# One reciprocal square root on ScalarE for a logarithm and an exponential, in an attention and MLP kernel under a planned order

## The chip, the cores and the metric

The kernel runs on one core of a Trainium2 chip. The metric is the device time of one execution in microseconds (us). Before the change the median of three runs is 662.1 us (660.76 to 663.17).

## The reference

A complex linear attention is followed by an MLP. There are 4 batches of 8 heads, 768 steps and a head width of 48. The transition of each step is a complex number per element, scaled so that its magnitude is at most 0.999:

```python
mag = np.sqrt(a_re * a_re + a_im * a_im)
scale = np.minimum(mag, 0.999) / (mag + 1e-06)
a_re_n, a_im_n = (a_re * scale, a_im * scale)
for t in range(S):
    new_re = ar * S_re - ai * S_im          # S_re, S_im: 48 x 48 per head
    new_im = ar * S_im + ai * S_re
    S_re, S_im = (new_re + k[t] v[t]^T, new_im)
    y[t] = q[t] @ S_re
x = y as 3072 tokens x 384
out = gelu(x @ w_in) @ w_out                # w_in 384 x 2048, w_out 2048 x 384
```

## The kernel before

The recurrence is worked out in chunks. The running products of the transitions are needed for every step. They are computed on 128 lanes, in 24 slices of 8 rows (9 rows in the last slice of a group). The slices form four groups, `lanes0` to `lanes3`, of 4, 4, 8 and 8 slices. A row is 48 numbers, so a slice's tile is 128x384, or 128x432 with 9 rows.

A slice has two phases. In phase a, `squares_a` squares both parts into `tab` (a ring of one buffer), their sum is made in `sum_of` (by TensorE for slices 1 to 5, otherwise by VectorE), `logs` makes the reciprocal magnitude r from the sum and the square of r, and `normalise` improves r by one Newton step and scales the transitions. Then `scan` multiplies the rows one after the other: two VectorE instructions per row, `tt` and `bt`. In phase b, one slice later, `squares_b`, `sum_of` and `logs` make the reciprocal squared magnitude of the products, and `towards` and `against` multiply keys and queries by the products into `xt`. `xt` goes to DRAM (`kq`) and comes back in another layout (`kqn`) for `unit`, which does the attention of 128 steps of a batch on TensorE (`att`) and makes a 128-token piece of the MLP's input `xT`. There are 24 units.

Both MLP weights come as 64-bit floats. Each is cut into 16 pieces of 128x384, and `weights` turns a piece into two 32-bit halves (`wi_hi`, `wi_lo`, `wo_hi`, `wo_lo`): on VectorE six instructions or so through `wh` and `raw`, on ScalarE a square and a sign with sums (checks of the range) and two copies, on TensorE three matmuls. `block` is the MLP on 2 or 3 units at a time, nine of them; it walks over 16 pieces f of the hidden layer: nine matmuls into `ph`, two Gelus on ScalarE (`gh`, `gf`), a subtraction on VectorE (`gl`), and matmuls into `po`.

No engine's order is written out by hand. All steps go into a `Plan`. `natural` ranks each step by the work that still hangs on it, plus a constant of its kind (`MORE`), where each VectorE step of a slice's scan counts `WL`-fold along the chain of scans. `forward` simulates the engines with fixed costs and takes the step of the highest rank that is ready; `BIAS` leans the choice where a step may run on one of two engines (`both`, `either`). `order` repeats this up to four times with ranks taken from a backward pass and keeps the shortest plan. `issue` then writes every engine's instructions in that order, and each engine works through its own list strictly in it. The lines of the profile are therefore nearly all L429, the line that records a step, and groups are told apart by tile names.

ScalarE needs the table set of a function loaded. `TABLES` names the set of each function for the plan; `issue` loads the set at L427 where it changes, L422 loads the first one, and the loads before Gelu have L429.

The change touches `TABLES`, `FIRST_TABLE`, `WL`, `MORE`, `BIAS` and `logs`.

Of the kernel before, what the change touches and what calls it, by code (L numbers as in the profile page):

```python
# [15 lines left out]
AF = mybir.ActivationFunctionType  # L16
# [66 lines left out]
ENTER, LEAVE = dict(narrow=0.09), dict(narrow=0.2, turn=0.075)  # L83
STAY = 1.0
COLD, WARM = 3.0, 4.0
TABLES = {AF.Ln: "natural_log_exp_and_others", AF.Exp: "natural_log_exp_and_others", AF.Gelu: "gelu"}
FIRST_TABLE = TABLES[AF.Ln]
NEAR = 0.076
LOCK = True
NGA, NGB = 6, 5  # L90
# [4 lines left out]
EARLIER, N_RAW, N_KP = 1, 4, 2  # L95
PASSES = 4
N_A = 4
WL = 4.532

MORE = dict(lanes0=483.83, lanes1=-1595.06, lanes2=-3639.85, lanes3=-3453.18, weights=-1624.01, units=-66.21, blocks=-85.66)  # L100
BIAS = dict(vector=-0.82, scalar=-1.94, gpsimd=0.93, sync=-6.23)


class Step:
# [8 lines left out]
class Plan:  # L113
# [57 lines left out]
    def add(self, calls):  # L171
# [4 lines left out]
        for call in calls:  # L176
# [9 lines left out]
            for x in tuple(call[2]) + tuple(call[3].values()):  # L186
                step.table = TABLES.get(x, step.table) if isinstance(x, AF) else step.table
            for x, writes in [(x, False) for x in ins] + [(x, True) for x in outs]:
# [85 lines left out]
    def natural(self):  # L274
# [4 lines left out]
        for i in range(len(steps) - 1, -1, -1):  # L279
# [9 lines left out]
            rest[i] = t  # L289
        return [t + MORE[s.kind] for t, s in zip(rest, steps)]  # L290

    def forward(self, rank):
# [6 lines left out]
        free = dict.fromkeys(FIXED, 0.0)  # L299
        table = FIRST_TABLE  # L300
        channel, flight = dict.fromkeys(FIXED, 0.0), []
# [5 lines left out]
        while len(order) < len(steps):  # L307
            best = None
            for e, waiting in pool.items():
# [8 lines left out]
                if len(steps[i].options) > 1:  # L318
                    ends = {o: max(free[o], ready[i], port[other[o]] if o in steps[i].port else 0.0) + c + BIAS[o] for o, (_, c) in steps[i].options.items()}
                    if ends[e] > min(ends.values()) + 1e-9:  # L320
# [99 lines left out]
    def issue(self):  # L420
        table = FIRST_TABLE
        self.nc.scalar.preload_act_table_set(table)  # L422
        for s in self.order():
            if s.table and s.table != table:
                table = s.table
                if table != "gelu":
                    self.nc.scalar.preload_act_table_set(table)  # L427
            for engine, name, args, kw in s.calls:
                getattr(getattr(self.nc, engine), name)(*args, **kw)  # L429
# [10 lines left out]
def lanes_and_chunks(ctx, tc, flags, a_lanes, x_lanes, v_units, w_in, w_out, out):  # L440
# [5 lines left out]
    P = Plan(nc, loose=[flags])  # L446
# [12 lines left out]
    sgn, tiny, low_w, sj = (by_partition[:, i:i + 1] for i in range(4))  # L459
# [82 lines left out]
    tiles, xs = {}, {}  # L542
# [59 lines left out]
    def logs(sb, sa):  # L602

        with P.together():
            if sb is not None:
                P.scalar.activation(tiles[sb]["te"], tiles[sb]["b2"], AF.Ln, bias=tiny)
            if sa is not None:
                P.scalar.activation(tiles[sa]["tb"], tiles[sa]["a2"], AF.Ln, bias=tiny)
            if sb is not None:
                P.scalar.activation(tiles[sb]["te"], tiles[sb]["te"], AF.Exp, scale=-1.0)  # L610
            if sa is not None:
                P.scalar.activation(tiles[sa]["tb"], tiles[sa]["tb"], AF.Exp, scale=-0.5)
        if sa is not None:
            P.scalar.activation(tiles[sa]["tc"], tiles[sa]["tb"], AF.Square, accum_out=flags[:, sa:sa + 1])

# [76 lines left out]
    def lanes_begin():  # L692
        for s in range(N_A):
            load_a(s)
        load_x(0)
        load_x(1)
        squares_a(0)
        logs(None, 0)
        normalise(0)
        squares_a(1)  # L700
        logs(None, 1)

    def tick(s):
# [10 lines left out]
        with P.work(part=f"a{s}"):  # L714
            if ahead is not None:
                squares_a(ahead)
            if g == 0:
                if back is not None:
                    logs(back, None)
                if ahead is not None:  # L720
                    logs(None, ahead)
            elif back is not None or ahead is not None:
                logs(back, ahead)
# [367 lines left out]
    def ticks(g):  # L1091
        P.chain["vector"] = "lanes", WL
        with P.work(f"lanes{g}"):
            for s in range(end):
                if slices[s][0] == g:
                    tick(s)
        P.chain.pop("vector")
# [255 lines left out]
```

## Time and profile before

| | us |
|---|---|
| median of three runs (lowest, highest) | 662.1 (660.76, 663.17) |
| span of the profiled execution | 659.6 |
| TensorE matmul busy | 614.1 (93%) |
| TensorE weight load busy | 563.8 (85%) |
| VectorE busy | 484.1 (73%) |
| ScalarE busy | 434.1 (66%) |
| GpSimd busy | 26.1 (4%) |

The span runs from the first instruction to the last; what lies around it is in the runs and not in the span, 2.5 us against the median. Busy TensorE time is that of pipelined matmuls whose ends are modelled. All times in the trace are from the start of the span. PE is TensorE, PEld its weight loads, DVE VectorE, ACT ScalarE, POOL GpSimd, SP SyncE.

### The profile page before, as it was taken

The page shows a single profiled execution, that of the slowest core. Times are in us where ns is not written, and L with a number is a line of the kernel's source. Part 1 is how long each engine was busy: PE and PEld are TensorE (multiplying, and loading weights), DVE is VectorE, ACT ScalarE, POOL GpSimd, SP SyncE. Part 2 cuts the span into 40 slices and gives each one's busy share as a digit, 9 for nine tenths or more (in the row PEclk, how much of TensorE's full clock was granted, in tenths as well). Part 3 has the DMA queues.
Part 4 walks back from the last instruction along what each step waited for, and adds up shares of the span by engine and source line. Part 5 has one row for each costly group of instructions (what it writes and reads, how often), then busy time and mean ns, then how long its engine had stood idle before and what let it go on. Part 6 is the DMA issues. An engine that isn't in the chain of part 4 may idle for free.

```text
span 659.6 us, 13997 instructions
## 1 busy us (share of the span) xinstructions
PE 614.1 (93%) x5154; PEld 563.8 (85%) x5154; DVE 484.1 (73%) x1204; ACT 434.1 (66%) x1107; POOL 26.1 (4%) x74
## 2 busy tenths in 40 slices
PE   4655499999999999999999999999999999999995
PEld 2322277988789999999999999999999999999995
DVE  6999999999999999999989999656334424232211
ACT  8976699999998979787476997535442422232332
POOL 1000100002000000120000000020000000000000
PEclk9787699999999999999999999999999999999999
DMA  9366876668266456687889966487444132110000
GB/s 322 119 158 161 256 225 212 185 196 258 71 197 173 116 135 177 163 173 158 198 198 219 230 157 166 116 167 169 104 88 88 50 64 46 34 51 15 25 1 27
DMA packets 210442, 93.51 MB, mean 142 GB/s; under 512 B 167744, under 2 KB 202688, under 8 KB 210368
## 3 DMA queue, kind: packets, MB, share of 16 engines
q1 hardware_dynamic: 210368, 92.57, 54.6%
q8 instruction: 41, 0.67, 0.4%
q14 instruction: 33, 0.27, 0.1%
HBM read 63.11 MB, written 25.69 MB: 135 GB/s over the span
## 4 chain that ended last, share of the span: by engine, by line
PE 70%; ACT 9%; DVE 9%; issue 2%; DMA 1%; SPq 0%; DVEq 0%; ACTq 0%
PE po L429 27%; PE ph L429 26%; PE att L429 17%; DVE a L429 2%; ACT a L429 1%; DVE tt L429 1%; ACT tab L429 1%; ACT L429 1%; ACT L427 1%; DVE xt L429 1%; ACT gh L429 1%; DVE bt L429 1%; ACT gf L429 1%; DMA raw<-in_w_pieces_dram 1%; ACT square L429 1%
## 5 line engine op out<-in xcount | busy, mean ns | idle before, releaser
L429 PE MATMUL ph<-xT,wi_hi 128*128 128x384 f32 (+1 forms) x864 | 209.2, 324 | 0.0
L429 DVE TENSOR_TENSOR gl<-gf,gh 128x384 fp32r<-128x384 f32 (+1 forms) x144 | 73.7, 512 | 126.4 <-ACT gf L429 126.0
L429 ACT ACTIVATE gh<-ph 128x384 fp32r<-128x384 f32 (+1 forms) x144 | 65.8, 457 | 149.6 <-PE ph L429 149.2
L429 PEld LDWEIGHTS ph<-xT,wi_hi 128*128 128x128 f32 x864 | 154.3, 188 | 2.2 <-ACT gf L429 0.2
L429 PE MATMUL ph<-xT,wi_lo 128*128 128x384 f32 (+1 forms) x432 | 137.3, 318 | 0.0
L429 PE MATMUL po<-wo_hi,gh 128*128 128x384 f32 x384 | 132.5, 345 | 0.9 <-ACT gh L429 0.7
L429 PE MATMUL po<-wo_lo,gh 128*128 128x384 f32 x384 | 129.7, 338 | 0.0
L429 PE MATMUL po<-wo_hi,gl 128*128 128x384 f32 x384 | 92.5, 342 | 0.0
L429 PEld LDWEIGHTS ph<-xT,wi_lo 128*128 128x128 f32 x432 | 81.3, 188 | 0.1
L429 PEld LDWEIGHTS po<-wo_hi,gh 128*128 128x128 f32 x384 | 72.1, 188 | 3.0 <-ACT gh L429 2.0
L429 PEld LDWEIGHTS po<-wo_lo,gh 128*128 128x128 f32 x384 | 72.5, 189 | 0.0
L429 DVE TENSOR_TENSOR tt<-bt,a 128x192 f32<-128x192 f32 x192 | 67.3, 350 | 0.5
L429 PEld LDWEIGHTS po<-wo_hi,gl 128*128 128x128 f32 x384 | 65.9, 188 | 1.6 <-DVE gl L429 0.7
L429 ACT ACTIVATE gf<-ph 128x384 f32<-128x384 f32 (+1 forms) x144 | 65.4, 454 | 2.5 <-DVE gl L429 2.5
L429 DVE TENSOR_TENSOR bt<-tt 128x96 f32<-128x96 f32 x192 | 48.1, 250 | 0.5
L429 PEld LDWEIGHTS att<-qT,kp 96*64 96x64 f32 (+1 forms) x512 | 39.4, 165 | 2.4 <-issue 1.5
L429 PE MATMUL att<-qT,kp 96*64 96x64 f32 (+1 forms) x512 | 41.0, 250 | 0.0
L429 DVE TENSOR_TENSOR kp<-att,causal 128x512 f32<-128x512 f32 x40 | 27.5, 687 | 9.5 <-PE att L429 9.4
L429 ACT ACTIVATE a<-tab 128x384 f32<-128x384 f32 (+1 forms) x48 | 25.6, 534 | 9.3 <-DVE tab L429 9.2
L429 PE MATMUL po<-wh,ident_r 128*128 128x384 f32 x48 | 22.0, 541 | 9.4 <-DVE wh L429 9.3
L429 PE MATMUL att<-tab,ident_r 128*128 128x384 f32 (+1 forms) x20 | 14.8, 896 | 13.6 <-ACT tab L429 13.6
L429 ACT ACT_TABLE_LOAD x21 | 26.9, 1283 | 0.3
(154 smaller groups left out, 992.9 us busy)
## 6 DMA issues: line engine op xcount, KB each, us to landing
kqn<-kq SPq DMA_DIRECT2D x96, 128.0 KB, 3.2
xt<-in_x_lanes_dram SPq DMA_DIRECT2D x24, 384.0 KB, 4.4
kq<-xt SPq DMA_DIRECT2D x48, 192.0 KB, 3.5
a<-in_a_lanes_dram SPq DMA_DIRECT2D x20, 384.0 KB, 3.4
raw<-in_w_pieces_dram SPq DMA_DIRECT2D x16, 384.0 KB, 4.1
raw<-in_moe_w_out_dram SPq DMA_DIRECT2D x16, 384.0 KB, 4.3
vn<-in_v_units_dram SPq DMA_DIRECT2D x24, 256.0 KB, 3.7
kqn<-kq SPq DMA_DIRECT2D x8, 768.0 KB, 5.7
```

What stands on the lines that cost most here:

```text
L427: self.nc.scalar.preload_act_table_set(table)
L429: getattr(getattr(self.nc, engine), name)(*args, **kw)
```

## The change

In `logs`, the reciprocal magnitude r of phase a was exp(-0.5 ln s), s being the sum of squares, and the reciprocal squared magnitude of phase b was exp(-ln s). Now ScalarE's function for the reciprocal square root is applied to s once: for phase a that is r, and for phase b its square is taken with another pass. The square of r in phase a with its sum into `flags` stays as it was. The table set of these functions changes with them. The constants of the plan (`WL`, `MORE`, `BIAS`) have new values, so that the order of all engines is made anew.

```diff
-TABLES = {AF.Ln: "natural_log_exp_and_others", AF.Exp: "natural_log_exp_and_others", AF.Gelu: "gelu"}
-FIRST_TABLE = TABLES[AF.Ln]
+TABLES = {AF.Abs_reciprocal_sqrt: "abs_reciprocal_sqrt_and_small", AF.Gelu: "gelu"}
+FIRST_TABLE = TABLES[AF.Abs_reciprocal_sqrt]
...
-WL = 4.532
-
-MORE = dict(lanes0=483.83, lanes1=-1595.06, lanes2=-3639.85, lanes3=-3453.18, weights=-1624.01, units=-66.21, blocks=-85.66)
-BIAS = dict(vector=-0.82, scalar=-1.94, gpsimd=0.93, sync=-6.23)
+WL = 7.070
+
+MORE = dict(lanes0=836.74, lanes1=-1334.97, lanes2=-1535.50, lanes3=-2379.12, weights=-1352.49, units=-293.87, blocks=-358.94)
+BIAS = dict(vector=0.64, scalar=-0.09, gpsimd=4.04, sync=-6.23)
...
         with P.together():
             if sb is not None:
-                P.scalar.activation(tiles[sb]["te"], tiles[sb]["b2"], AF.Ln, bias=tiny)
+                P.scalar.activation(tiles[sb]["te"], tiles[sb]["b2"], AF.Abs_reciprocal_sqrt, bias=tiny)
             if sa is not None:
-                P.scalar.activation(tiles[sa]["tb"], tiles[sa]["a2"], AF.Ln, bias=tiny)
+                P.scalar.activation(tiles[sa]["tb"], tiles[sa]["a2"], AF.Abs_reciprocal_sqrt, bias=tiny)
             if sb is not None:
-                P.scalar.activation(tiles[sb]["te"], tiles[sb]["te"], AF.Exp, scale=-1.0)
-            if sa is not None:
-                P.scalar.activation(tiles[sa]["tb"], tiles[sa]["tb"], AF.Exp, scale=-0.5)
+                P.scalar.square(tiles[sb]["te"], tiles[sb]["te"])
         if sa is not None:
             P.scalar.activation(tiles[sa]["tc"], tiles[sa]["tb"], AF.Square, accum_out=flags[:, sa:sa + 1])
```

## Rows read from the trace of the kernel before

**Rows 1.** The page: busy tenths of the span in 40 equal slices.

```profile
PE   4655499999999999999999999999999999999995
DVE  6999999999999999999989999656334424232211
```

**Rows 2.** Busy time by stretch; columns in the first line, x is a count.

```profile
core 0: us, PE busy (x) PEld busy (x) DVE busy (x) ACT busy (x) POOL busy (x), PEclk, DMA share, GB/s
0.00:83.00 83.00, 45.40 (x94) 23.66 (x95) 73.81 (x202) 64.24 (x158) 6.38 (x33) 0.80 0.68 205
83.00:128.00 45.00, 44.97 (x622) 37.24 (x622) 43.54 (x125) 44.22 (x132) 0.13 (x1) 0.99 0.72 215
128.00:160.00 32.00, 31.96 (x313) 28.11 (x311) 31.02 (x81) 31.75 (x79) 6.20 (x13) 1.00 0.75 221
200.00:660.00 460.00, 452.29 (x3668) 442.29 (x3666) 296.71 (x694) 255.59 (x642) 13.38 (x27) 1.00 0.50 118
```

**Rows 3.** Chain that ended last, to 165 us: start, length, what.

```profile
80.63 2.93 PE att L429 x4
...
100.68 0.69 DVE kp L429
...
128.40 0.39 ACT gf L429
...
129.62 1.28 ACT L427
...
130.91 0.62 ACT a L429
...
160.71 0.96 PE po L429 x4
```

**Rows 4.** Groups of ScalarE, whole span: count, busy us, mean ns, idle before.

```profile
L429 ACT ACTIVATE tab<-tab 128x384 f32<-128x384 f32 (+1 forms) x24 | 12.5, 521 | 0.3
L429 ACT ACTIVATE tab<-tab,by_partition 128x384 f32<-128x384 f32 x16 | 9.7, 606 | 0.2 <-DVE tab L429 0.2
L429 ACT ACTIVATE gh<-ph 128x384 fp32r<-128x384 f32 x96 | 47.0, 490 | 105.0 <-PE ph L429 104.6
L429 ACT ACT_TABLE_LOAD x21 | 26.9, 1283 | 0.3
L427 ACT ACT_TABLE_LOAD x20 | 25.7, 1283 | 0.3
```

**Rows 5.** Timeline of slice 4's phase a, ScalarE and VectorE: start, length, what.

```profile
49.79 0.58 ACT L429 ACTIVATE tab<-att,by_partition 128x384 f32<-128x384 f32 x1 [2.62 <-PE att L429]
50.40 0.52 ACT L429 ACTIVATE tab<-tab 128x384 f32<-128x384 f32 x1
50.83 0.83 ACT L429 ACTIVATE a<-bt 128x768 f32<-128x768 f32 x1
52.19 0.56 DVE L429 TENSOR_TENSOR a<-att,a 128x384 f32<-128x384 f32 x1 [0.79 <-ACT a L429]
57.25 0.84 ACT L429 ACTIVATE tab<-a 128x768 f32<-128x768 f32 x1 [2.11 <-issue]
```

**Rows 6.** Groups of ScalarE from 83 to 160 us: phase a's exponentials, table loads.

```profile
L429 ACT ACTIVATE tab<-tab 128x384 f32<-128x384 f32 (+1 forms) x4 | 2.1, 526 | 0.0
L427 ACT ACT_TABLE_LOAD x3 | 3.8, 1283 | 0.1
```

**Rows 7.** Waits of TensorE's weight loads, 128 to 200 us: us in total, times, longest.

```profile
PEld po L429 <- DVE gl L429: 0.7, 2, 0.6
```

**Rows 8.** Timeline of SyncE and TensorE where the first unit starts.

```profile
75.78 1.01 SPq L429 DMA_DIRECT2D kqn<-kq  x2
84.80 1.14 PE L429 MATMUL ph<-vn,kqn 64*64 64x48 f32 x32
```

**Rows 9.** Groups of VectorE, forms apart: a scan's two instructions and the products.

```profile
L429 DVE TENSOR_TENSOR tt<-bt,a 128x192 f32<-128x192 f32 x192 | 67.3, 350 | 0.5
L429 DVE TENSOR_TENSOR bt<-tt 128x96 f32<-128x96 f32 x192 | 48.1, 250 | 0.5
```

## The prediction

> **What bounds the kernel now.** I read the busy tenths first, to cut the span into stages; then the busy time by stretch, to see which engine is full in each; then the chain that ended last, to see who hands over to whom; and last the timeline of one slice, to see what the removed instruction holds up. The tenths show TensorE full from the sixth slice (some 83 us) to the end, while VectorE is full only in the first two thirds of the span, at most [rows 1]. So there are three stages. In the lead-in, 0 to 83 us, TensorE has only 45.40 us of work, VectorE 73.81 and ScalarE 64.24 [rows 2]. In the ramp, 83 to 160 us, all three are full: TensorE 44.97 of 45 and 31.96 of 32 us, VectorE 43.54 and 31.02, ScalarE 44.22 and 31.75 [rows 2]. After 200 us TensorE is busy 452.29 of 460 us and VectorE and ScalarE have 163 and 204 us to spare [rows 2].
>
> The chain says the same. It passes over to TensorE at 80.63 us, to VectorE at 100.68, to ScalarE at 128.40, and at 160.71 it reaches TensorE, where it mostly stays [rows 3]. TensorE's work is the same before and after, since no matmul is touched. The end can only move by when the first unit starts, and by what TensorE waits for in the ramp.
>
> **What is removed, and its price.** Phase a loses one ScalarE pass per slice, the exponential `tab<-tab`: 24 of 521 ns on the mean, 12.5 us busy [rows 4]. Consecutive ScalarE instructions overlap: the exponential of slice 4 starts at 50.40 and the next one at 50.83 us, so a pass takes 0.43 us of the engine's queue [rows 5]. For 24 slices that is 24 x 0.43 = 10.3 us of ScalarE. What waits for the result itself is spared more: the logarithm starts at 49.79 with 0.58 us, the exponential could start only at 50.40 and its end is at 50.92, so a waiting reader gains 0.52 + 0.03 = 0.55 us [rows 5].
>
> Phase b loses nothing: a logarithm becomes a reciprocal square root and an exponential becomes a square, one for one. No row shows the reciprocal square root. I bound it by a Gelu on 128x384, 490 ns, and the logarithm with its bias read per partition, 606 ns, and take 606, because its operands are the same [rows 4]. At 490 ns each would save 0.12 us more, in the lead-in some 0.5 us on the four slices of the first group. Upwards the nearest row is a pass over twice as many elements, 0.84 us [rows 5]; that would take 0.23 us per slice back, some 0.9 us on the four. Both stay in the range. The Trainium skill says that every function runs at one element per cycle ("ScalarE: Activation LUTs", "What ACT_TABLE_LOAD costs"), and its formula for a bias by pointer gives an estimate of 600 ns for 384 elements. That agrees with the logarithm's 606 ns and would leave the sum as it is.
>
> Loads of a table set, 20 at L427 and 21 at L429 of 1283 ns each [rows 4], come from the alternation of slices and Gelus, which stays. How many the new order has can't be read from a row. Of the 20 only three lie between 83 and 160 us [rows 6], and behind that ScalarE has time; I cost a change of their number at nothing. If the new order puts one pair more into the ramp, it costs 2 x 1.28 = 2.6 us of an engine that is full there.
>
> **Lead-in.** Seven of the 24 exponentials lie before 83 us: 24, less the four from 83 to 160 us [rows 6], less the 13 behind. `tab` has one buffer, so the next slice's squares wait until this slice's last reader is done: those of slice 5 start at 57.25 us after 2.11 us in which ScalarE had nothing it could run [rows 5]. This loop of latencies, some 11 us per slice, holds the exponential once. The first unit needs slices 0 to 3 and their scans. So if the loop binds, four slices give 4 x 0.43 to 4 x 0.55 = 1.7 to 2.2 us, and slices 4 and 5, which VectorE's list mixes into the scan of slice 3, give a little more: VectorE stands still for 0.79 us for slice 4 alone [rows 5], of which 0.55 can vanish. The other bound is nothing: behind the first slice of the tenths VectorE is almost never idle (9 and 9 again [rows 1]), its work isn't reduced, and where the loop isn't last a shorter one only lets VectorE take weights in another order. All seven at 0.55 would be 3.9 us. I take 1.7 + 0.7 = 2.4 us, close to the loop's value, because the loop's idle time is seen in the rows of slice 4 on both engines.
>
> **Ramp.** Four exponentials, 4 x 0.43 = 1.7 us of a full ScalarE, which carries the chain from 128.40 to 160.71 us [rows 3, 6]. TensorE's waits there for ScalarE and VectorE are small single ones: the largest entry of the waits is 0.7 us in two waits [rows 7]; it has other work in its list. So between 0 and 1.7 us, and I take 0.8. The work can't be traded for VectorE's: steps that may go to either engine can move, but ScalarE becomes free by only 1.7 of 77 us there.
>
> After 160 us, 13 exponentials go from an engine that waits 105.0 us for TensorE before its Gelus [rows 4]. That is worth nothing; the cover is TensorE's own queue, and if it were gone a pass would cost 0.43 us.
>
> **The new order.** Every engine's list is made anew, so every wait can move. Two places price it. On the good side, the first unit's transfer is issued at 75.78 us by SyncE, yet its first matmul starts at 84.80, behind a sum for a later slice whose four matmuls take 2.93 us from 80.63 us [rows 3, 8]. An order without that sum in front of the unit starts up to 2.9 us earlier, if the data has landed. On the bad side, VectorE's work for a slice of a later group may come ahead of weights that the first block waits for: a slice's scan is (67.3 + 48.1) / 24 = 4.8 us [rows 9]. I take zero for the middle and keep -2.9 and +4.8 for the range.
>
> **Sum.** -2.4 - 0.8 + 0 = -3.2 us. The profiled span is 659.6 us and would become 656.4; the median of the runs lies 2.5 us above that span, so 662.1 - 3.2 = 658.9 us.
>
> **Rivals.** *VectorE binds, nothing comes of it.* For it: VectorE is busy 73.81 of the first 83 us and 74.56 of the next 77 [rows 2], and most of the rest lies in the first slice of the tenths [rows 1]. If the lead-in ends when VectorE's list ends, only its own idle time can shrink, by 0.55 us for slice 4 and little else. Against it: that idle time exists and is caused by the removed pass [rows 5]. Time: 662.1 - 0.6 = 661.5.
>
> *The order improves too.* For it: the sum in front of the first unit [rows 8], and a shorter phase a makes that sum ready earlier. Against it: nothing binds the plan to it. Time: 658.9 - 2.9 = 656.0, and down to 662.1 - 3.9 - 1.7 - 2.9 = 653.6 with all bounds.
>
> *Weights come later (slower).* Scans count 7.07-fold instead of 4.53-fold along their chain, so that later groups' scans rank higher beside the weights. VectorE is full in the ramp, and the first block can't go on without its piece of the weights. One scan ahead of a needed piece costs 4.8 us there; two cost 9.6. The price decides from 3.2 us, that is from two thirds of a scan, on: 658.9 + 4.8 = 663.7 for one and 668.5 for two. The diff's constants lean that way for the third group (`lanes2` rises by 2104, `weights` by 272), though not for the second (`lanes1` by 260). Against it: the ranks of later passes come from the backward pass, not from these constants. The chain in VectorE's hands from 100.68 to 128.40 us [rows 3] is where it would show.
>
> *The new table set lacks a small function.* Then each square, sign or copy among the slices would need a load on either side, 2.6 us. On four slices of the lead-in that is 10.4 us on the loop, 658.9 + 10.4 = 669.3. Against it: before, squares, signs and copies run under both sets, and the loads of the two lines are as many as these two sets' alternation, 20 and 21 [rows 4]. The Trainium skill says that cheap functions are in every set as filler ("ScalarE: Activation LUTs", "Table sets: the hidden batching unit"); by that this rival can't occur, and the rows agree as far as two sets go. The same page puts a switch at 2.66 us with its drain; the trace shows the next instruction 0.01 us behind the load's 1.28, at 130.91 after 129.62 [rows 3], so I price a load at 1.28.
>
> **How the numbers follow.** This kernel's measurement can tell about 0.3%, 2.0 us, from no change: faster is below 660.1, slower above 664.1. The forecast has 0.42 (its own range 657 to 660), the better order 0.18, VectorE binding 0.25, later weights 0.12, the table set 0.03. Faster 0.42 + 0.18 = 0.60. Same 0.25 and that part of the later weights that one scan makes, 0.03, is 0.28. Slower 0.09 + 0.03 = 0.12. The likeliest case gives 658.9. The range goes down to 653.6 with the bounds of lead-in, ramp and order taken, and up to one scan late, 663.7, with the dearer reciprocal square root, 0.9, on it: 664.6. At the lower end the cheaper one takes 0.5 more: 653.1.
>
> **What would show it.** Right: 24 fewer ScalarE passes on `tab`, ScalarE's busy time 12 us lower, the first unit's matmuls 2 to 3 us before 84.80, and the stretch from there to the end as long as before, within 1 us. `tab`'s loop should be near 10.5 instead of 11 us. Wrong: the first unit at 84 to 85 us (VectorE binds), TensorE idle for weights between 90 and 160 us (weights late), far more loads than 41, or reciprocal square roots much over 0.6 us. If the end moves more than the first unit's start does, the gain came from the order and not from the removed pass.

## The result and the profile after

The changed kernel is slower, by half a per cent: 3.5 us between the medians, where the forecast was a gain of 3.2 us.

| | before | after |
|---|---|---|
| median of 16 runs each, same chip | 662.88 us | 666.41 us |
| lowest, highest | 659.9, 667.25 | 665.2, 667.79 |
| ratio, with its 95% interval | | 1.0051 [1.0036, 1.0066] |
| span of the profiled execution | 659.6 us | 664.9 us |

The page of after, busy time of each engine over the span:

```profile
PE 613.3 (92%) x5154; PEld 564.8 (85%) x5154; DVE 490.0 (74%) x1213; ACT 412.5 (62%) x1012; POOL 25.4 (4%) x73
```

Groups of ScalarE in after, whole span (count, busy us, mean ns of one, idle before):

```profile
L429 ACT ACT_TABLE_LOAD x21 | 26.9, 1283 | 0.4
L427 ACT ACT_TABLE_LOAD x20 | 25.7, 1283 | 0.4
L429 ACT ACTIVATE tab<-tab,by_partition 128x384 f32<-128x384 f32 x16 | 9.7, 604 | 0.1
```

The edit did what the diff says. The group `tab<-tab` of [rows 4] is gone with all its 24 passes. The reciprocal square root takes 604 ns where the logarithm took 606 [rows 4], and there are as many table loads as before. ScalarE has 21.6 us less to do, and yet the kernel takes longer.

Where the time went can be read in two cuts. The first cut is at the first unit's first matmul, which is at 84.80 us before [rows 8] and at 80.03 in after; the first line is the sum for a later slice that stands ahead of it (timeline of TensorE: start, length, what):

```profile
75.11 2.93 PE L429 MATMUL att<-a,ident_r 128*128 128x384 f32 x4 [2.84 <-ACT a L429]
...
80.03 0.70 PE L429 MATMUL att<-ident_r,kqn 128*96 128x128 f32 x8
80.66 1.13 PE L429 MATMUL ph<-vn,kqn 64*64 64x48 f32 x32
```

The second cut is at TensorE's last matmul, the sum of the checks, at 653.31 us before and at 657.20 in after. Busy time by stretch with these cuts, before (columns as in [rows 2]):

```profile
0.00:84.80 84.80, 47.20 (x99) 24.48 (x99) 75.60 (x208) 65.44 (x161) 6.38 (x33) 0.80 0.69 208
84.80:653.31 568.51, 566.73 (x5056) 539.26 (x5056) 408.36 (x996) 368.68 (x947) 19.71 (x41) 1.00 0.53 133
```

The same view of after:

```profile
0.00:80.03 80.03, 44.35 (x98) 24.06 (x99) 72.89 (x202) 62.77 (x152) 6.93 (x33) 0.77 0.71 213
80.03:657.20 577.17, 568.73 (x5055) 540.65 (x5054) 416.94 (x1011) 349.68 (x861) 18.50 (x40) 1.00 0.53 132
```

TensorE does the same work on either side of the cut, 99 and 98 matmuls ahead of it and 5056 and 5055 behind. So the three parts can be compared:

- The lead-in is 4.77 us shorter (84.80 to 80.03).
- The stretch from the first unit to the last matmul is 8.66 us longer (568.51 to 577.17).
- The tail from there to the end of the span is 1.41 us longer (6.29 to 7.70).

-4.77 + 8.66 + 1.41 = +5.30 us, the difference of the spans. In the long stretch TensorE stood idle for 568.51 - 566.73 = 1.78 us before and for 577.17 - 568.73 = 8.44 us in after. Its busy time is 2.0 us longer for the same matmuls; part of that is the fall of the clock shown below.

By stage, after (columns as in [rows 2]):

```profile
83.00:128.00 45.00, 43.65 (x638) 35.66 (x637) 43.55 (x120) 44.32 (x138) 0.13 (x1) 1.00 0.69 209
128.00:160.00 32.00, 28.59 (x236) 26.07 (x235) 30.57 (x82) 29.36 (x69) 6.31 (x13) 1.00 0.66 187
160.00:200.00 40.00, 38.92 (x465) 32.22 (x464) 35.26 (x99) 34.49 (x85) 0.00 (x0) 0.96 0.49 137
```

Most of the new idle time lies in the ramp: 1.35 us from 83 to 128 us and 3.41 us from 128 to 160, where [rows 2] have 0.03 and 0.04. ScalarE isn't full there any more (29.36 of 32 us, before 31.75). The waits of TensorE from 128 to 200 us name the largest piece (us in total, times, longest):

```profile
PE att L429 <- DMA kqn<-kq: 2.6, 1, 2.6
PE po L429 <- ACT gh L429: 1.1, 2, 0.8
PE att L429 <- ACT kp L429: 0.6, 1, 0.6
```

A unit waits for its keys and queries, which come back from DRAM. Before, the whole list of that stretch held only a wait of 0.5 us for `gh`. No single wait makes the loss: from the first unit to the end of the last block the listed waits of TensorE add up to 0.7 us before and to 7.2 us in after. The timeline of TensorE in after there:

```profile
155.93 0.51 PE L429 MATMUL po<-wo_hi,gl 128*128 128x384 f32 x2
159.09 0.75 PE L429 MATMUL att<-ident_r,kqn 128*96 128x128 f32 x8 [2.65 <-DMA kqn<-kq]
159.68 1.15 PE L429 MATMUL po<-wh,ident_r 128*128 128x384 f32 x2
160.10 1.05 PE L429 MATMUL po<-wi_hi,minus 128*128 128x384 f32 x1
```

And the five microseconds behind it, by stretch, with the granted clock as the third number from the end:

```profile
155.00:160.00 5.00, 2.35 (x16) 1.71 (x16) 4.43 (x12) 3.54 (x11) 0.00 (x0) 1.00 0.83 255
160.00:165.00 5.00, 5.00 (x23) 3.97 (x21) 3.06 (x9) 3.87 (x10) 0.00 (x0) 0.66 0.72 216
```

The wait has a second price: behind it the granted clock is 0.66, that is, about two thirds of these 5 us at the lower level of 1.2 GHz. A `wi_hi,minus` matmul takes 1.05 us there and 0.64 at full clock. A fall doesn't follow every such wait: in e4 below, which has the order of after, TensorE waits 2.0 us for the same `kqn`, and the clock stays at 1.00 behind it:

```profile
PE att L429 <- DMA kqn<-kq: 2.0, 1, 2.0
160.00:165.00 5.00, 2.98 (x25) 2.47 (x24) 4.53 (x13) 4.70 (x15) 0.00 (x0) 1.00 1.09 350
```

Over the whole span the clock isn't what makes after slower: the mean granted clock of its sixteen executions is 0.968, that of the kernel before in the sets of runs beside the experiments 0.965 to 0.967.

The chain that ended last passes there through three transfers (start, length, what), where that of before passes from ScalarE to TensorE at 160.71 us [rows 3]:

```profile
142.07 5.97 DMA raw<-in_moe_w_out_dram
...
154.22 2.56 DMA kqn<-kq
156.79 9.38 DMA raw<-in_moe_w_out_dram
166.25 0.65 ACT square L429 x2
```

Two of them are pieces of the weights; the last is read by ScalarE at 166.25 us.

Another wait comes much later. From 290 to 410 us TensorE waits in after for VectorE's part of a unit's `xT`, which has no counterpart before:

```profile
PE att L429 <- DVE xT L429: 1.2, 1, 1.2
```

Of the kernels below, e4, e6 and e8, which have the order of after, have this wait too (1.6, 1.2 and 1.2 us); e3 and e3b, which have the old one, don't.

### The profile page after: what moved, and what is told of

It reads as the page before. It is cut to its first block, busy times and chain, and to the rows that moved or that the text cites. A ratio compares the mean times of both kernels' runs of the same rounds, so it can differ in the third digit from the quotient of the medians.

```text
span 664.9 us, 13900 instructions
## 1 busy us (share of the span) xinstructions
PE 613.3 (92%) x5154; PEld 564.8 (85%) x5154; DVE 490.0 (74%) x1213; ACT 412.5 (62%) x1012; POOL 25.4 (4%) x73
## 4 chain that ended last, share of the span: by engine, by line
PE 76%; DVE 9%; ACT 8%; DMA 3%; issue 2%; SPq 1%; DVEq 0%; ACTq 0%
PE po L429 30%; PE ph L429 28%; PE att L429 18%; DMA raw<-in_moe_w_out_dram 2%; DVE a L429 2%; ACT square L429 2%; ACT a L429 1%; DVE tt L429 1%; ACT tab L429 1%; DVE bt L429 1%; DVE tab L429 1%; DVE xt L429 1%; DVE wh L429 1%; SPq L429 1%; ACT L427 1%
## 5 line engine op out<-in xcount | busy, mean ns | idle before, releaser
L429 PE MATMUL po<-wh,ident_r 128*128 128x384 f32 x48 | 23.8, 580 | 9.8 <-DVE wh L429 9.8
L429 PE MATMUL att<-tab,ident_r 128*128 128x384 f32 (+1 forms) x20 | 12.4, 763 | 19.1 <-ACT tab L429 19.1
```

## The experiments

Two things changed at once, the function and the order of all lists. To separate them, the functions were exchanged while the lists are written, so that the order stays as it was planned, step for step. Every kernel was timed beside the kernel before on its chip. The ratio stands with its 95% interval. The three parts come from each kernel's profiled execution as above: start of the first unit's first matmul, from there to the last matmul, and from there to the end.

| kernel | median us | ratio to before | lead-in | stretch | tail |
|---|---|---|---|---|---|
| before | 662.9 to 664.0 | | 84.80 | 568.51 | 6.29 |
| after | 666.41 | 1.0051 [1.0036, 1.0066] | 80.03 | 577.17 | 7.70 |
| e3 old order, new function | 662.97 | 0.9992 [0.9968, 1.0016] | 82.60 | 568.19 | 6.71 |
| e3b the same again | 661.80 | 0.9971 [0.9954, 0.9989] | 84.34 | 568.44 | 6.42 |
| e4 new order, old function | 672.07 | 1.0145 [1.0115, 1.0176] | 83.17 | 577.81 | 8.12 |
| e5 old order, one pass more | 671.86 | 1.0117 [1.0095, 1.0139] | 86.02 | 573.98 | 6.40 |
| e1 new function, old constants | 670.63 | 1.0129 [1.0079, 1.0180] | 85.68 | 576.12 | 7.90 |
| e2 old function, new constants | 677.78 | 1.0228 [1.0190, 1.0266] | 81.64 | 584.72 | 8.34 |
| e7 new function, third constants | 664.65 | 1.0007 [0.9984, 1.0030] | 82.20 | 575.64 | 8.06 |
| e6 after, kqn issued earlier | 664.92 | 1.0019 [1.0003, 1.0035] | 81.85 | 575.82 | 8.23 |
| e8 e6, more on SyncE's list | 664.82 | 1.0009 [0.9992, 1.0027] | 81.72 | 574.50 | 8.18 |
| e9 e3 without the checks of weights | 660.56 | 0.9950 [0.9922, 0.9979] | 81.50 | 574.85 | 6.45 |
| e10 e3, a VectorE pass less per piece | 661.31 | 0.9948 [0.9922, 0.9974] | 82.78 | 569.98 | 6.64 |

The parts are those of one execution, and the lead-in varies: e3 and e3b are one kernel, and their first units start 1.74 us apart, with the stretch alike within 0.25 us. After, e6 and e8 have the same lists up to 148 us, and their first units start at 80.03, 81.85 and 81.72 us, so the 80.03 of after is an early one. The profiled executions of e6, e7 and e9 took 667.65, 667.64 and 664.61 us, 2.7 to 4.1 us above their medians, and those of e3 and e5 took 659.25 and 668.18, 3.7 us below. So differences are judged by the ratios, and the parts tell where they lie.

**The function alone, in the old order.** The plan is that of before; while steps are issued, the logarithm becomes the reciprocal square root, exp(-0.5 x) is left out and exp(-x) becomes a square:

```diff
-            for engine, name, args, kw in s.calls:
+            for engine, name, args, kw in one_pass(s.calls):
...
+        if AF.Ln in args:
+            args = tuple(AF.Abs_reciprocal_sqrt if x is AF.Ln else x for x in args)
+        if AF.Exp in args:
+            if kw["scale"] == -0.5:
+                continue
+            name, args, kw = "square", args[:2], {}
```

> The plan of the kernel before, step for step, with the reciprocal square root put in when the instructions are written: every engine's list is that of before, less 24 exponentials on ScalarE. Theory A (the removed pass helps, the new order costs more than it gives): the lead-in is 2 to 3 us shorter, the first unit's matmuls at 82 to 83 us instead of 84.80, and the time is 658 to 661 us against 662.9 of before, a ratio of 0.993 to 0.997. Theory B (the reciprocal square root itself is dearer than the logarithm, or its table set costs loads): slower than before, 664 to 667 us, with passes of tab from a sum at much over 0.61 us or more than 43 loads. Theory C (VectorE binds, the pass is worth nothing): 662 to 664 us.

> The old order with the new function once more, to narrow its interval: the first time gave a ratio of 0.9992 with an interval from 0.9968 to 1.0016. If the pass is worth what was forecast, 0.995 or below; if it is worth nothing in this order, 0.998 to 1.001.

Measured: 0.5 us less than before (663.42) in the first set of runs and 1.7 us less (663.48) in the second; only the second interval leaves 1 out. The first median lies in the range of theory C. The second ratio, 0.9971, lies between the two ranges expected for it. The stretch is 0.1 to 0.3 us shorter than that of before. So the pass that the forecast priced at 3.2 us is worth about 1 us in the old lists, and next to nothing of it lies behind the first unit. Busy time by stretch of e3:

```profile
82.60:650.79 568.19, 566.22 (x5056) 539.42 (x5056) 407.98 (x996) 362.56 (x930) 21.61 (x41) 1.00 0.53 133
```

TensorE's idle time is 1.97 us here and was 1.78 before. There was hardly anything left to win in this stretch.

**The order alone.** The plan is that of after, and the logarithm and both exponentials are put back while steps are issued:

```diff
+        if AF.Abs_reciprocal_sqrt in args:
+            first.append((engine, name, tuple(AF.Ln if x is AF.Abs_reciprocal_sqrt else x for x in args), kw))
+            scale = -1.0 if any(args[0] is x for x in squared) else -0.5
+            then.append((engine, "activation", (args[0], args[0], AF.Exp), dict(scale=scale)))
```

> The plan of the changed kernel, step for step, with the logarithm and the exponential put back when the instructions are written. Theory A: the order alone costs 6 to 7 us against before and the pass comes on top, 668 to 671 us, a ratio of 1.008 to 1.012. Theory B: the order is innocent, and the time is that of before or better, 658 to 663 us. Theory C: the order alone is the whole difference, 666 to 667 us, as the changed kernel has it.

Measured: 8.7 us more than before, with the old function, and above all three ranges expected. The order alone makes the kernel slower, and in this order the pass is worth 672.07 - 666.41 = 5.7 us, more than in the old one and more than the forecast. The stretch has 577.81 us, nearly as in after, and TensorE is idle for 9.86 us of it (8.44 in after): most of its loss is there with either function.

**One pass more, in the old order.** A copy of `tab` onto itself behind each exp(-0.5 x):

```diff
+        if AF.Exp in args and kw["scale"] == -0.5:
+            out.append((engine, "activation", (args[0], args[0], AF.Copy), {}))
```

> The kernel before in its own order, with one more pass over tab on ScalarE behind each of the 24 exponentials of phase a, a copy in place of some 0.5 us (the opposite of the change). If the loop of latencies over tab's one buffer sets the lead-in, the first unit starts 2 to 3 us later and the time is 665 to 667 us, a ratio of 1.003 to 1.006. If VectorE sets it and ScalarE has room, there is no difference, 662 to 664 us. If the order is one in which ScalarE's list is full to the brim in the ramp, as in the new order where the pass cost 5.7 us, 668 us or more.

Measured: 1.0117, 7.8 us by the ratio, the third of the cases expected. One pass more costs several times what one pass less gives. The first unit starts 1.2 us later, and in the stretch TensorE's idle time grows from 1.78 to 573.98 - 569.08 = 4.90 us; its waits for `gh`, which ScalarE writes, grow from 0.7 to 2.7 us. Busy time by stretch of e5:

```profile
86.02:660.00 573.98, 569.08 (x5055) 539.52 (x5054) 408.54 (x995) 376.69 (x963) 19.41 (x41) 1.00 0.53 131
```

That the lists suit only the durations for which they were laid out is my reading; no run shows it by itself.

**Constants and functions exchanged.** In e1 the code of after is planned with the constants of before; in e2 the code of before with the constants of after; in e7 the code of after with a third set:

```diff
-WL = 7.070
+WL = 3.94398
-MORE = dict(lanes0=836.74, lanes1=-1334.97, lanes2=-1535.50, lanes3=-2379.12, weights=-1352.49, units=-293.87, blocks=-358.94)
+MORE = dict(lanes0=-292.0984, lanes1=-1565.8031, lanes2=-5431.9781, lanes3=-2629.4233, weights=-1624.0100, units=-52.6754, blocks=-90.4173)
```

> The changed kernel with the constants of the plan of before; the order is made anew with them, since the costs of ScalarE's steps differ. If the new constants as such cause the loss: 657 to 661 us. If every newly made order is as likely to lose a few us in the ramp: anything from 657 to 670 us, and TensorE's waits between 100 and 200 us tell which.

> The kernel before with the new constants of the plan alone, so with a third order. If the new constants as such cause the loss: 668 to 672 us. If it is the one order that came out of them: anything from 660 to 672 us.

> The changed kernel with another set of constants of the plan, found for the new function; so one more newly made order. If an order made for the shorter ScalarE can use the whole pass: 655 to 660 us. If a newly made order loses in the ramp what it gains in the lead-in, as the changed kernel does: 663 to 668 us.

Measured: 1.0129, 1.0228 and 1.0007. The first two lie above their ranges, and e7 is in the second of its own. Each set of constants goes with the code for which it is in the diff; exchanged, either way, the kernel is 7 to 15 us slower than before. The third set starts the first unit at 82.20 us and gives the gain back in a stretch of 575.64, in an execution 3.0 us above its median. In these profiles after, e1, e2, e4 and e7 have stretches of 575.6 us or more, against 568.2 to 568.5 for before and e3; for e7 the median speaks for some 3 us less, an estimate.

**The transfers of keys and queries.** SyncE issues transfers in the order of its list. In after, the `kqn` that TensorE waits for stands behind transfers of `xT` (timeline of SyncE: start, length of the issue, what):

```profile
148.02 2.11 SPq L429 DMA_DIRECT2D xT<-x  x1
150.23 0.54 SPq L429 DMA_DIRECT2D raw<-in_w_pieces_dram  x1
150.82 3.36 SPq L429 DMA_DIRECT2D xT<-x  x4
154.22 0.58 SPq L429 DMA_DIRECT2D kqn<-kq  x1
154.85 0.59 SPq L429 DMA_DIRECT2D xT<-x  x1
155.48 0.58 SPq L429 DMA_DIRECT2D kqn<-kq  x1
```

In e6 five `xT` transfers and the load of `xt` were moved behind these two `kqn` and the last piece of the weights; nothing else changes:

```diff
+        late = [out[n] for n in (873, 880, 885, 891, 902)]
+        out = [s for s in out if s not in late]
...
+        return out[:k] + late + out[k:]
```

> The changed kernel with one edit in SyncE's list, at 150 us: the transfers of units 4 and 5 (kqn) and the last piece of the weights go ahead of five small transfers of xT and the load of a slice; all else is in the order of the changed kernel. If SyncE's list is what starves TensorE between 140 and 170 us: kqn lands at 156 to 158 us instead of 159.05 and 164.07, the last piece at about 161 instead of 166.17, the wait of 2.65 us of TensorE for kqn goes, and the time is 661.5 to 664 us, a ratio of 0.998 to 1.001 to before (the changed kernel has 1.0051). If VectorE and ScalarE, full in the ramp, are what is late and the transfers only follow them: 665.5 to 667 us.

Measured: 1.0019, 2.1 us less than after by the ratios and 1.5 by the medians, between the two ranges. TensorE's wait for `kqn` from 128 to 200 us is 2.6 us in after; in e6, and in e8 below, which has the same edit, it is

```profile
PE att L436 <- DMA kqn<-kq: 0.4, 1, 0.4
PE att L439 <- DMA kqn<-kq: 1.2, 1, 1.2
```

Not all of the shorter wait in e6 is the edit's. Counted from the first unit's first matmul, the first `kqn` lands 79.02 us later in after, 78.96 in e6 and 78.00 in e8: in e6 it isn't earlier, and TensorE itself is later, for a reason that the next experiment shows. So the edit gains by the ratios 2.1 us in e6 and 2.8 in e8, of a loss of 3.4, each known to about 1.5 us: the late transfers are a cause of some half of the loss or more, and how much of it is `kqn` and how much the last piece of the weights isn't shown. No more can be had from the place of these two `kqn` in SyncE's list: in after the data is in DRAM (`kq` landed) at 151.55 us and the first `kqn` goes out at 154.22, in e6 these are 155.69 and 155.89, and it lands 4.9 us later.

**More instructions on SyncE's list.** After the last matmul the tail is 7.70 us and more in every kernel with a new order, and 6.71 and less in those with the old one. One idea was that it depends on where the end of SyncE's list falls. e8 is e6 with 15 empty instructions on SyncE:

```diff
+            if n == 2600:
+                for _ in range(15):
+                    self.nc.sync.nop(nofuse=True)
```

> As e6_new_order_kqn_first, with 15 empty instructions on SyncE in the middle of its list, while it idles, so that its list has the 745 instructions of the old order instead of some 730. At the end of the program SyncE stands still between two semaphore events for 1.2 to 1.3 us in the new order and not in the old one. If that is where in its instructions the end falls: the stop goes or moves, and the time is some 1.2 us below that kernel's ratio of 1.0019, about 1.000. If it is something else: the stop stays, 1.002.

Measured: the tail stays, 8.18 us, and the ratio is 1.0009, between the two times expected. But this run doesn't test the idea: the 15 instructions aren't in the trace. SyncE has 731 instructions in e8 as in e6, both pages count 13900 in all, and the stop stands at the same place. The other traces speak for the idea. The last 21 instructions of SyncE only close the program, and they come behind a wait of 2.1 to 3.6 us that every kernel has. In all seven kernels with a longer tail SyncE has 730 to 742 instructions, so that the 724th is one of these 21, and right before it SyncE stands still, for 1.2 us in after and 2.2 at most (e1). In those with the shorter tail it has 745 or 749, the 724th comes before the last 21, and there is no such stop among them. In after that is 1.2 of the 1.4 us. Why SyncE stops there stays open, and no run changed the count alone.

But e6 and e8 have the same lists in the ramp, and their stretches differ by 1.32 us. The timeline of TensorE shows where. In e6:

```profile
109.88 0.34 PE L436 MATMUL po<-wo_lo,minus 128*128 128x384 f32 x1
111.53 0.67 PE L436 MATMUL ph<-xT,wi_hi 128*128 128x256 f32 x2 [1.31 <-DMA xT<-x]
112.00 0.41 PE L436 MATMUL ph<-xT,wi_lo 128*128 128x256 f32 x1
112.21 1.48 PE L436 MATMUL att<-m,ident_r 96*128 96x384 f32 x2
113.49 1.49 PE L436 MATMUL att<-m,other_half 96*128 96x384 f32 x2
...
116.00 0.68 PE L436 MATMUL att<-kp,vn 64*64 64x64 f32 x16
```

And in e8:

```profile
109.77 0.34 PE L439 MATMUL po<-wo_lo,minus 128*128 128x384 f32 x1
111.33 0.48 PE L439 MATMUL ph<-xT,wi_hi 128*128 128x256 f32 x2 [1.22 <-DMA xT<-x]
111.64 0.28 PE L439 MATMUL ph<-xT,wi_lo 128*128 128x256 f32 x1
111.76 0.81 PE L439 MATMUL att<-m,ident_r 96*128 96x384 f32 x2
112.41 0.81 PE L439 MATMUL att<-m,other_half 96*128 96x384 f32 x2
...
114.14 0.68 PE L439 MATMUL att<-kp,vn 64*64 64x64 f32 x16
```

TensorE stands still for 1.31 and 1.22 us, at the same place in its list. In e6 the matmuls behind it run at the lower clock, a pair taking 1.48 us, and from 111.53 to 116.00 us it gets through what takes from 111.33 to 114.14 in e8: 4.47 against 2.81 us. One such fall of the clock costs 1.66 us. The windows of 110 to 115 us grant 0.66 and 1.00. What decides whether a stand is followed by a fall can't be read from these two.

**Which other engine is full.** If the pass gives little because VectorE or ScalarE is full anyway, then taking other work from one of them should tell which. e9 is e3 without the square and sign of each piece of the weights on ScalarE; e10 is e3 without one of VectorE's instructions per piece:

```diff
+        if engine == "scalar" and args and args[0].tensor.name.startswith("square"):
+            continue
```

```diff
+        if engine == "vector" and kw.get("scalar1") == 0xFF800000:
+            continue
```

> The old order with the new function and without the checks of the weights: their squares and signs with sums on ScalarE, 64 passes and 64 reads of sums, are left out, so that ScalarE has far more room in the lead-in and the ramp. If ScalarE still limits the old order once the exponential is gone: 650 to 657 us, a ratio of 0.98 to 0.99. If it no longer does, and VectorE or the transfers do: the 0.997 to 0.999 that the order has with the checks, at most 2 us less.

> The old order with the new function and with one VectorE pass less for each of the 32 pieces of the weights: the mask of the exponent is left out, so the low halves of the weights are wrong. That is 0.27 us of VectorE's list each, 15 of them before 83 us and 15 until 160 us. If VectorE binds the lead-in: the first unit 3 to 4 us earlier and 655 to 659 us, a ratio of 0.988 to 0.994. If it doesn't: 661 to 663 us.

Measured: 0.9950 and 0.9948, some 1.4 to 2.9 us below the two runs of e3 by the ratios; against e3b, 1.4 and 1.5 us, that is within the uncertainty of some 2 us. Both medians lie above the ranges for a bound by ScalarE or VectorE. In e9 ScalarE falls to 31.01 of 45 us busy in the stretch from 83 to 128 us:

```profile
83.00:128.00 45.00, 44.20 (x578) 36.74 (x578) 40.45 (x114) 31.01 (x85) 0.13 (x1) 0.92 0.65 190
```

and TensorE stays at 44.20, with its clock at 0.92 in this execution, so that e9's stretch of 574.85 us isn't typical of it. That both help little speaks against one of the two engines alone as the bound of the ramp. Taking 128 instructions from ScalarE (33 us busy over the span), or 32 from VectorE (6 us), gives a few tenths of a per cent at most.

## Why the prediction was wrong, point by point

*What bounds the kernel.* This held in the main. The end moved only by the first unit's start and by TensorE's waits behind it, except for the tail, which I hadn't counted and which took 1.4 us. What I didn't draw from [rows 2] was the sign: with TensorE busy 44.97 of 45 us and 31.96 of 32, and 1.78 us idle in 568.51, a change of the lists could take hardly anything away behind the first unit and could add a lot.

*The pass removed.* The instructions went as said. ScalarE's busy time falls by 21.6 us and not 12, because the new order also puts other steps on VectorE, which has 490.0 instead of 484.1 us (of the small products `m<-m,gg` ScalarE does 8 instead of 64). With the old order (e3) it falls by 434.1 - 425.8 = 8.3 us, against 10.3 worked out.

*Reciprocal square root and table loads.* Right: 604 ns and 606, 41 loads and 41. The rival "the new table set lacks a small function" fell with that.

*Lead-in, -2.4 us (0 to -3.9).* In the profile of after the first unit starts 4.77 us sooner, more than the 2 to 3 us I named as the sign. `tab`'s loop from slice 4 to 5 went from 11.38 us (45.87 to 57.25) to 9.43 (43.05 to 52.48), against 10.5 forecast; the function alone (e3) gives 9.97 and the order alone (e4) 10.01, so the loop did give way. But the early start comes from function and order together, and from the execution: with the old function the same order starts it at 83.17 us, the old order with the new function at 82.60 and 84.34, and the lists of after in e6 and e8 at 81.85 and 81.72. To the end, in the old order, lead-in and ramp together came to about 1 us of the 3.2 that I summed. Its 0.7 us for slices 4 and 5 had only the 0.55 us of slice 4 behind it. For that order the term was mis-sized: nearer to my lower bound, and to the rival "VectorE binds", which gave 0.6 us. In the new order the same pass is worth 5.7 us, so its price isn't one number.

*Ramp, -0.8 us.* Mis-sized as well: 0.1 to 0.3 us in e3's stretch, within what two executions of one kernel differ by. TensorE's idle time, 1.78 us, left no more to gain.

*The new order, zero, bounds -2.9 and +4.8.* This is the step that failed, and it decides the sign. e4 shows the order alone at +8.7 us with the old function, and after lies 3.9 to 5.3 us above e3 (0.0059 and 0.0080 of the ratio). Zero was taken as the middle of two bounds, while the rows spoke for an uneven spread. Behind the first unit, a list under which TensorE stands still for 1.78 us is near its best; a newly made one can hardly better it there. My upper bound was one late scan. In its place stood several waits that no row of before shows: `kqn` 2.65 us with a fall of the clock behind it, `gh`, `xT` by DMA 0.8 us, `xT` by VectorE 1.2 us, and the tail.

*Rivals.* "Weights come later" had the right sign and nearly the right size (663.7 to 668.5 us), but not by its mechanism as far as the runs show: transfers in SyncE's list were late, those of keys and queries and the last piece of the weights, and no wait of TensorE names weights behind VectorE's scans. e6 moves both, so it doesn't tell them apart; the wait that shrank on TensorE is that for `kqn`. "VectorE binds" is close to what the pass does in the old order. "The order improves too" didn't come about: in after the sum still stands in front of the first unit, 2.93 us from 75.11 us, only earlier, and what the earlier start gained was given back in the ramp.

*The sign I had set for myself* was that the stretch from the first unit on stays within 1 us, and that otherwise the order is at work. It moved by 8.66 us, in e4 by 9.30 and in e3 by 0.07 to 0.32. That points to the order, and the exchange of functions bears it out.

What the runs settle: the loss comes from the order; the late transfers are some 1.5 to 2.8 of 3.5 us of it. Read from the profiles, without a run of its own: the wait for `xT` by VectorE, 1.2 us, and the stop of SyncE in the tail, 1.2 of its 1.4 us. Open: what makes SyncE stop.

The best of both is e3, the new function written into the old lists: 0.9992 and 0.9971 of before, and faster than after by 3.9 to 5.3 us by the ratios.

## What to carry to other kernels

When a change comes with a newly made order, price the two apart: write the new instruction into the old lists, and the old one into the new. Before you take zero for a new order, read how long the bounding engine stands still under the old one; where that is next to nothing, a new order can hardly gain in that stretch and can lose a lot. And a pass has a price only within an order: here, in the old one, its removal gave 1 us and one more cost 7.8, and in the new one its removal gave 5.7.

## What the runs showed of the hardware

- A wait of TensorE can cost twice. Behind a stand of 1.31 us the granted clock was 0.66 for the next stretch and 1.66 us were lost on top (e6); behind one of 1.22 us at the same place it stayed at 1.00 (e8). In after a fall to 0.66 stands behind the wait of 2.65 us for `kqn`; behind the same wait in e4, 2.0 us, there is none.
- One kernel's lead-in varies from execution to execution: e3 and e3b start their first unit at 82.60 and 84.34 us. TensorE's clock in that stage is far from even; the mean granted is 0.77 and 0.80 from 0 to 83 us in these two, and the one with the lower clock started earlier, so the mean clock doesn't explain it.
- The issue of a transfer by SyncE took 0.5 to 0.6 us for several in after, but 5.35 us for one piece of the weights, the one that the chain above passes through for 9.38 us; the same issue took 1.80 us in e6 and 3.36 in e4. The timeline of SyncE there:

```profile
156.79 5.35 SPq L429 DMA_DIRECT2D raw<-in_moe_w_out_dram  x1
```
- The longer tails go with the number of SyncE's instructions, which no run changed alone. In seven kernels it has 730 to 742 and stands still for 1.2 to 2.2 us right before the 724th (1.20 us in after, 1.26 in e6, 1.33 in e4); in those with 745 or 749 there is no such stop among its last 21, and the tail is 6.29 to 6.71 us instead of 7.70 to 8.34.
